# Idle transposes on TensorE around the first score tiles of an attention and two-layer feed-forward kernel

## The chip, the cores and the metric

The kernel runs on one core of a Trainium2 chip. The metric is the device time of one execution in microseconds (us), of which the median of three runs is given. TensorE (PE) does the matmuls, VectorE (DVE), ScalarE (ACT) and GpSimd (POOL) the elementwise work, and SyncE (SP) issues most of the DMAs.

## The reference, cut to what matters

```
q, k, v: (4, 8, 576, 64) f32
q_rot, k_rot = rotate(q), rotate(k)                   # rotary embedding
scores = 1/8 * q_rot @ k_rot.T
attn = exp(scores - max(scores));  attn /= sum(attn)
x = (attn @ v)  as (2304, 512)
g = x @ w_gate                                        # d_ff 1536
x = (silu(g) * (x @ w_val)) @ w_out
g = relu(x @ w_in2) ** 2                              # d_ff 2048
out = g @ w_out2
```

## The kernel before, in words

There are two parts. Part one computes the attention of 32 heads, taken in 16 pairs of heads (a pair is `g`, and `b, j = divmod(g, 4)` its batch and place), and slips in the first chunks of the feed-forward layer as filler matmuls. Part two is the rest of the two feed-forward layers, plain loops of matmuls. The change touches part one only.

For each pair, `add_prep` loads k and q (tile `rot`), multiplies them by the cosine and sine table (L493 for pair 0, L499 for the others) and adds the two halves (L495, L500). `add_kq` splits the rotated k and q into a high part and a rest (L529 to L547 for pair 0, L555 and L557 for the others) and, for pairs after the first, copies them into the operand tiles `kh`, `qa` and `qz` by 13 small DMAs from SP's queue (L569). `add_scores` makes nine score tiles of 128 queries: matmuls of 288 columns into the PSUM tile `s`, of which there are two (L589: four matmuls to each of the tiles 0 to 7, six to tile 8), a maximum on DVE (`nm`, L595), and an exponential on ACT into `p` (L597), which also frees `s`. `add_values` turns `p` by transposes on TensorE (128 x 128, into PSUM tile `pt`, L618), copies them out to `pc` on DVE or ACT (L612, L610), and multiplies by v into the PSUM tile `av`, of which there is one (L652, L655), in two halves: tiles 0 to 3, then 4 to 8. Then come the division by the sum and the split of x for the feed-forward layer. The filler matmuls are L730, the unpacking of the weights L237 to L242.

The order in which each engine does all this is written out ahead of time by a list scheduler inside the kernel, `Plan.order`. Each piece of work is added with an engine, an assumed duration, what it reads and writes, and a rank. At each step the lowest rank that is ready goes next on its engine, where ready goes by the assumed durations. On TensorE every piece has a mode, 0 for score tiles and fillers and 1 for transposes and the product with v, and `STAY` is added to the rank of a piece whose mode is not the last one's: as it is negative, this favours alternating. `Plan.order` also keeps an account of the TensorE clock: it doubles the assumed duration of a piece on TensorE unless enough columns (`COLUMNS`) were counted in the tick before. The chip then runs each engine's list in order, waiting only for real data.

A rank is the pair's number plus `rk(name, g)`, which adds `RANK[name]`, for the first pairs `RANK0` (g < 4) and `RANK1` (g < 2), and for pairs 0 and 1 an entry such as `s0` or `s1`.

Of the kernel before, what the change touches and what calls it, by code (L numbers as in the profile page):

```python
# [18 lines left out]
NR = 64  # L19


RANK = dict(ld=204.044, rope=131.839, k=-43.228, lo=-160.592, dup=314.157, v=-3.533, s=-129.888, mx=-88.9, ex=261.988, pt=-38.854, hi=266.287, av=521.86, rec=59.628, x=402.058, out=453.471, fin=-509.939, scale=-72.768, w=-420.559, dw=352.51, fill=-125.25, sp=-470.346, wl=-348.575, dwl=322.979, df=2.639, r01=-1095.946, r11=-1461.728, r00=-1011.214, r10=-1194.454, k00=-943.413, o00=-768.952, l00=-1080.687, q00=-1037.859, m00=-1368.159, z00=-979.186, k01=-1295.916, o01=-849.303, l01=-1007.3, q01=-1150.876, m01=-747.26, z01=-1157.79, k10=-1334.655, o10=-963.986, l10=-785.158, q10=-957.376, m10=-1162.732, z10=-508.046, k11=-1305.768, o11=-882.245, l11=-858.73, q11=-571.838, m11=-1040.058, z11=-893.411, c0=-569.247, c1=-938.134, rope1=392.215, k1=55.939, lo1=73.053, dup1=-319.318, s0=113.672, s1=262.807, mx0=-214.829, mx1=-239.888, ex0=-79.738, ex1=169.647, pt0=125.887, pt1=-295.963, hi0=103.851, hi1=38.71, av0=492.403, rec0=-133.459, x0=59.381, out0=101.915, scale0=371.475, fin0=-57.497, v1=-56.063)
SHARE = (1,)
RANK0 = dict(rope=-3.842, hi=-1.283, rec=-0.102, out=1.765, scale=3.431, av=6.868, ld=-3.342, dup=0.135, fin=4.672, v=1.694, x=1.078, csq=-0.229, mx=-16.145, k=0.021, lo=5.707, s=-4.387)
RANK1 = dict(ld=2.027, rope=-0.905, k=-15.778, lo=-1.529, v=0.489, s=-520.975, mx=1.596, ex=1.472, pt=-1.685, hi=-4.396, av=0.978, rec=0.97, x=-3.819, fin=-5.258, scale=0.809, csq=4.36)
PB = 10
PC = 6
QB = 4
# [19 lines left out]
class Plan:  # L48
# [7 lines left out]
    HOP = 200  # L56
    HOPS = {("ACT", "DVE"): 152, ("DVE", "ACT"): 128, ("ACT", "PE"): 227, ("ACT", "Pool"): 170, ("Pool", "ACT"): 170, ("Pool", "DVE"): 170}
    SWITCH = 0
    STAY = -578.97

    def __init__(self, places):
        self.places = dict(places)
# [130 lines left out]
def tile_attention_moe_moe2(  # L193
# [13 lines left out]
    nc = tc.nc  # L207
# [147 lines left out]
    with ExitStack() as p1:  # L355
# [8 lines left out]
        plan = Plan(places)  # L364
# [28 lines left out]
        def pe(cols):  # L393
            return cols / 2.4 + 14
# [176 lines left out]
        def add_scores(g):  # L571
            P = pair[g]
            P["p"] = [buf("p", [128, S], bufs=PB) for _ in range(NT)]
            P["sums"] = sums = ssum[g % 2]
            kh, kl, qa, qz = P["kh"], P["kl"], P["qa"], P["qz"]
            for x in range(NT):
                t, h = divmod(x, 2)
                at = g + x / NT
                ps, nm, p = buf("s", [128, 2, 512], bufs=2, pool=pp), buf("nm", [128, 1], bufs=8, pool=sm), P["p"][x]
                for i in range(2):  # L580
                    def mm(i=i, t=t, h=h, ps=ps):
                        c = slice(i * HS, (i + 1) * HS)
                        if t < 4:
                            (_, qc), (_, zc) = (q_at(h, t * 128, t * 128 + 128, z)[0] for z in (NR, 0))
                            prods = [(qa()[:, qc], kh()[:, h, c]), (qz()[:, zc], kl()[:, c])]
                        else:
                            prods = [(qa()[:, NM:NM + 128], kh()[:, 0, c]), (qa()[:, S:S + 128], kh()[:, 1, c]), (qz()[:, NM:NM + 128], kl()[:, c])]
                        for y, (a, w) in enumerate(prods):
                            nc.tensor.matmul(ps()[:, i, :HS], lhsT=a, rhs=w, start=y == 0, stop=y == len(prods) - 1)  # L589
                    nq = {int(t * 128 >= HS), int(min(t * 128 + 127, S - 1) >= HS)}  # L590
                    hs_ = (h,) if t < 4 else (0, 1)
                    rd = [(qa, (h_, y, n)) for h_ in hs_ for y in range(2) for n in nq] + [(qz, (h_, n)) for h_ in hs_ for n in nq]
                    rd += [(kh, (h_, y, i)) for h_ in hs_ for y in range(2)] + [(kl, (h_, i)) for h_ in range(2)]
                    plan.add("PE", pe(HS) * (2 if t < 4 else 3), mm, rd, [ps], at + rk("s", g), cols=HS * (2 if t < 4 else 3))
                plan.add("DVE", 755, lambda ps=ps, nm=nm: nc.vector.tensor_reduce(  # L595
                    out=nm(), in_=ps()[:, :, :HS], axis=AX.XY, op=ALU.max, negate=True), [ps], [nm], at + rk("mx", g))
                plan.add("ACT", 930, lambda x=x, ps=ps, nm=nm, p=p: nc.scalar.activation(  # L597
                    p().rearrange("p (a b) -> p a b", a=2), ps()[:, :, :HS], AF.Exp,
                    bias=nm(), accum_out=sums()[:, x:x + 1]), [ps, nm], [p, (sums, x)], at + rk("ex", g), hold=-100)
# [159 lines left out]

        add_prep(0)  # L760
        add_kq(0)
        for g in range(1, NG):
            add_prep(g)
        for g in range(NG):
            if g:
                add_kq(g)
            add_scores(g)
            add_values(g)
            if g // NP < NSP:
                add_spill(g)  # L770
# [158 lines left out]
```

## Time and profile before

| what | value |
|---|---|
| median of three runs | 1136.91 us (1135.49 to 1137.95) |
| profiled execution: its own time | 1136.43 us |
| profiled execution: its span | 1134.5 us |
| PE busy | 1106.2 us, 98% of the span |
| DVE, ACT, POOL busy | 591.1, 474.4, 482.3 us |
| first and last score matmul start | 12.1 us, 327.3 us |

The span is the stretch from the first to the last instruction of the profiled execution; its own time is 1.9 us more. A matmul's time in a row is from its start to its end in the pipeline, so rows of consecutive matmuls overlap: how fast they follow each other is read from the differences of their starts. "Idle before" is the time for which an engine had nothing running, and the releaser named is what ended it.

### The profile page before, as it was taken

The page shows a single profiled execution, that of the slowest core. Times are in us where ns is not written, and L with a number is a line of the kernel's source. Part 1 is how long each engine was busy: PE and PEld are TensorE (multiplying, and loading weights), DVE is VectorE, ACT ScalarE, POOL GpSimd, SP SyncE. Part 2 cuts the span into 40 slices and gives each one's busy share as a digit, 9 for nine tenths or more (in the row PEclk, how much of TensorE's full clock was granted, in tenths as well). Part 3 has the DMA queues.
Part 4 walks back from the last instruction along what each step waited for, and adds up shares of the span by engine and source line. Part 5 has one row for each costly group of instructions (what it writes and reads, how often), then busy time and mean ns, then how long its engine had stood idle before and what let it go on. Part 6 is the DMA issues. An engine that isn't in the chain of part 4 may idle for free.

```text
span 1134.5 us, 16644 instructions
## 1 busy us (share of the span) xinstructions
PE 1106.2 (98%) x6348; PEld 929.3 (82%) x6348; DVE 591.1 (52%) x974; ACT 474.4 (42%) x985; POOL 482.3 (43%) x380
## 2 busy tenths in 40 slices
PE   4999999999999999999999999999999999999998
PEld 4777788888878888888888888888888888888887
DVE  8778787776664647446355373551144246233212
ACT  6776676666554423122132133443352224223121
POOL 6986784855115324123132145652252234224121
PEclk9999999999999999999999999999999999999999
DMA  9866667564419413012021030120031012000112
GB/s 301 229 194 184 178 166 216 146 158 134 109 49 355 130 45 93 19 32 81 1 75 38 12 101 1 44 68 1 19 94 38 1 57 75 1 1 1 66 29 75
DMA packets 61248, 102.44 MB, mean 90 GB/s; under 512 B 11120, under 2 KB 37488, under 8 KB 60272
## 3 DMA queue, kind: packets, MB, share of 16 engines
q1 hardware_dynamic: 59904, 96.46, 28.5%
q0 software_dynamic: 576, 4.19, 1.0%
q8 instruction: 50, 0.82, 0.3%
q10 hardware_dynamic: 688, 0.72, 0.2%
q14 instruction: 30, 0.25, 0.1%
HBM read 67.17 MB, written 12.06 MB: 70 GB/s over the span
## 4 chain that ended last, share of the span: by engine, by line
PE 89%; DMA 3%; POOL 2%; SPq 2%; DVE 1%; ACT 1%; issue 1%; ACTq 0%; POOLq 0%; DVEq 0%
PE mm L279 23%; PE mm L278 23%; PE mm L280 23%; PE s L589 6%; PE av L652 5%; PE pt L618 5%; PE mm L730 3%; SPq L569 2%; POOL rot L499 1%; DMA qa<-rot 1%; POOL rot L500 1%; ACT p L597 1%; PE av L655 1%; PE pt L674 0%; DMA cs<-in_rope_dram 0%
## 5 line engine op out<-in xcount | busy, mean ns | idle before, releaser
L293 POOL TENSOR_TENSOR h<-s,h 128x512 fp32r<-128x512 f32 (+1 forms) x80 | 96.2, 1203 | 181.5 <-ACT h L292 181.4
L293 POOL TENSOR_TENSOR h<-hf,h 128x512 fp32r<-128x512 f32 (+1 forms) x54 | 66.9, 1238 | 150.7 <-ACT h L292 150.6
L312 DVE TENSOR_TENSOR s<-r,mm 128x512 f32<-128x512 f32 (+1 forms) x80 | 50.6, 633 | 146.6 <-POOL h L293 75.2
L589 PE MATMUL s<-kh,qa 128*128 128x288 f32 x320 | 104.5, 351 | 22.2 <-DVE qa L547 12.1
L595 DVE TENSOR_REDUCE nm<-s 128x1 f32<-128x576 f32 x144 | 106.2, 752 | 15.9 <-PE s L589 13.1
L279 PE MATMUL mm<-wo,h 128*128 128x512 f32 (+1 forms) x292 | 111.5, 386 | 0.0
L618 PE MATMUL pt<-ident,p 128*128 128x128 f32 (+1 forms) x720 | 108.7, 274 | 1.6 <-ACT pc L610 1.1
L597 ACT ACTIVATE p<-s,nm 128x576 f32<-128x576 f32 x144 | 105.5, 734 | 11.2 <-DVE nm L595 8.8
L278 PE MATMUL mm<-wo,h 128*128 128x512 f32 (+1 forms) x292 | 110.1, 386 | 0.0
L280 PE MATMUL mm<-wo,h 128*128 128x512 f32 (+1 forms) x292 | 93.9, 386 | 0.0
L310 ACT ACTIVATE r<-mm 128x512 f32<-128x512 f32 (+1 forms) x80 | 43.9, 549 | 119.2 <-PE mm L280 118.5
L242 POOL TENSOR_TENSOR wi<-wa,wi 128x512 fp32r<-128x512 f32 x36 | 47.2, 1312 | 108.0 <-ACT wi L241 108.0
L618 PEld LDWEIGHTS pt<-ident,p 128*128 128x128 f32 (+1 forms) x720 | 86.4, 135 | 8.1 <-ACT pc L610 1.9
L589 PEld LDWEIGHTS s<-kh,qa 128*128 128x128 f32 x320 | 60.2, 195 | 35.5 <-ACT p L597 16.2
L301 DVE SCALAR_TENSOR_TENSOR th<-th,mm 128x512 f32<-128x512 f32 (+1 forms) x54 | 33.9, 627 | 105.6 <-ACT th L299 105.5
L589 PE MATMUL s<-kl,qz 128*128 128x288 f32 x288 | 85.0, 302 | 0.0
L239 DVE SCALAR_TENSOR_TENSOR wp<-wa,wp 128x512 uint32<-128x512 uint32 x62 | 53.4, 862 | 57.9 <-ACT wa L237 57.8
L292 ACT ACTIVATE h<-s 128x512 fp32r<-128x512 f32 (+1 forms) x80 | 47.2, 590 | 77.3 <-DVE s L312 77.3
L652 PE MATMUL av<-pc,v 128*64 128x256 f32 x640 | 76.1, 384 | 0.0
L612 DVE COPY pc<-pt 128x512 f32<-128x512 f32 (+1 forms) x96 | 64.7, 686 | 21.8 <-PE pt L618 21.6
L292 ACT ACTIVATE h<-hf 128x512 fp32r<-128x512 f32 (+1 forms) x54 | 31.5, 584 | 98.5 <-DVE hf L304 98.0
L280 PE MATMUL mm<-h,wo 128*128 128x512 f32 (+1 forms) x200 | 72.6, 369 | 0.0
(216 smaller groups left out, 2814.9 us busy)
## 6 DMA issues: line engine op xcount, KB each, us to landing
raw<-in_moe_w_out_dram SPq DMA_DIRECT2D x26, 512.0 KB, 3.5
rot<-in_k_dram SPq DMA_DIRECT2D x15, 576.0 KB, 5.0
rot<-in_q_dram SPq DMA_DIRECT2D x15, 576.0 KB, 3.8
kh<-rot SPq DMA_DIRECT2D x60, 144.0 KB, 2.6
raw<-in_moe_w_in_dram SPq DMA_DIRECT2D x16, 512.0 KB, 3.6
raw<-in_moe_w_gate_dram SPq DMA_DIRECT2D x10, 512.0 KB, 3.5
raw<-in_moe_w_val_dram SPq DMA_DIRECT2D x10, 512.0 KB, 3.5
qa<-rot SPq DMA_DIRECT2D x30, 144.0 KB, 2.7
```

Source lines behind the costliest of these rows:

```text
L239: lambda: nc.vector.scalar_tensor_tensor(out=p(), in0=a(), scalar=3, in1=p(), op0=ALU.logical_shift_left, op1=ALU.bitwise_or),
L278: nc.tensor.matmul(ps, lhsT=ah, rhs=bh, start=first, stop=False)
L279: nc.tensor.matmul(ps, lhsT=ah, rhs=bl, start=False, stop=False)
L280: nc.tensor.matmul(ps, lhsT=al, rhs=bh, start=False, stop=last)
L292: nc.scalar.activation(h[:, 0, :n], hf[:, :n], AF.Copy)
L293: nc.gpsimd.tensor_tensor(out=h[:, 1, :n], in0=hf[:, :n], in1=h[:, 0, :n].bitcast(F32), op=ALU.subtract)
L589: nc.tensor.matmul(ps()[:, i, :HS], lhsT=a, rhs=w, start=y == 0, stop=y == len(prods) - 1)
L595: plan.add("DVE", 755, lambda ps=ps, nm=nm: nc.vector.tensor_reduce(out=nm(), in_=ps()[:, :, :HS], axis=AX.XY, op=ALU.max, negate=True), [ ...
L597: plan.add("ACT", 930, lambda x=x, ps=ps, nm=nm, p=p: nc.scalar.activation(p().rearrange("p (a b) -> p a b", a=2), ps()[:, :, :HS], AF.Exp ...
L612: nc.vector.tensor_copy(dst()[:kk], pt()[:kk, :n])
L618: nc.tensor.matmul(pt()[:kk, off + n * 128:off + n * 128 + 128], lhsT=p()[:, c * 128:c * 128 + kk], rhs=ident, is_transpose=True)
L652: nc.tensor.matmul(av()[h * 64:h * 64 + 64, 0:256], lhsT=vt()[:, h, c], rhs=pcs[c]()[:, h * 256:h * 256 + 256], start=c == 0, stop=c == 4)
```

## The change

Two things change. First, `add_idle` adds transposes on TensorE whose results nobody reads. Seven pieces of four of them (28) have the rank -1e5, so they go first on TensorE; they read the first part of pair 0's k tile (`src`), so they can start when that part has been multiplied (L493), and they write one of the two `s` slots. After each of the first four maxima (the loop is over `range(4)`), two pieces of two transposes (16 in all) are listed, writing the `av` slot; the maximum is named as what they read for the order alone, as no operand of theirs is that tile. Second, all ranks are other numbers, some entries of `RANK0` and `RANK1` are gone or new, and `STAY` goes from -578.97 to -439.551, so the order on every engine may differ throughout part one.

```diff
-RANK = dict(..., rope=131.839, s=-129.888, mx=-88.9, pt=-38.854, ..., s0=113.672, s1=262.807, mx0=-214.829, ..., pt0=125.887, pt1=-295.963, rope1=392.215, ...)
+RANK = dict(..., rope=103.217, s=-108.397, mx=-81.407, pt=-50.164, warm=-28.837, ..., s0=119.219, s1=304.557, mx0=-196.999, ..., pt0=139.231, pt1=-361.862, rope1=347.578, ...)
 SHARE = (1,)
-RANK0 = dict(rope=-3.842, ..., mx=-16.145, ..., s=-4.387)
-RANK1 = dict(..., rope=-0.905, ..., s=-520.975, mx=1.596, ..., pt=-1.685, ...)
+RANK0 = dict(rope=50.938, ..., s=-1.154, ex=-1.301)
+RANK1 = dict(..., rope=-0.45, ..., s=-0.067, ex=-3.837, pt=-3.587, ...)
+WARM = 2
...
-    STAY = -578.97
+    STAY = -439.551
...
+                P.setdefault("nm", []).append(nm)
...
         add_prep(0)
         add_kq(0)
+
+        idle = buf("s", [128, 2, 512], bufs=2, pool=pp), buf("av", [128, 512], pool=pp)
+        src = pair[0]["rot"][1]
+
+        def add_idle(t, n, rd, rank):
+            def mm():
+                for i in range(n):
+                    out = idle[t]()[:, 128 * (i % 4):128 * (i % 4) + 128] if t else idle[t]()[:, 0, 128 * (i % 4):128 * (i % 4) + 128]
+                    nc.tensor.matmul(out, lhsT=src()[:, 0, 0:128], rhs=ident, is_transpose=True)
+            plan.add("PE", 110 * n, mm, [(src, 0)] + rd, [idle[t]], rank, mode=1, cols=256 * n)
...
             add_scores(g)
+            if g == 0:
+                for i in range(7):
+                    add_idle(0, 4, [], -1e5)
+                for x in range(4):
+                    for i in range(WARM):
+                        add_idle(1, 2, [pair[0]["nm"][x]], x / NT + RANK["s"] + RANK0["s"] + RANK["warm"])
             add_values(g)
```

## Rows read from the trace of the kernel before

**Rows 1.** Page, busy time of each engine (share of the span) and instructions.
```profile
PE 1106.2 (98%) x6348; PEld 929.3 (82%) x6348; DVE 591.1 (52%) x974; ACT 474.4 (42%) x985; POOL 482.3 (43%) x380
```

**Rows 2.** Waits of PE: engine, line, releaser; us in total, times, longest.
```profile
PE s L589 <- DVE qa L547: 12.1, 1, 12.1
PE s L589 <- ACT p L597: 9.7, 15, 2.4
PE pt L618 <- ACT pc L610: 1.1, 2, 0.8
```

**Rows 3.** Windows by stage: length, then busy us (instructions) of each engine.
```profile
12.13:20.06 7.93, 4.77 (x17) 3.92 (x17) 7.48 (x12) 5.41 (x15) 6.45 (x4) 1.00 1.10 351
20.06:26.00 5.94, 5.94 (x24) 5.61 (x25) 5.35 (x9) 4.51 (x11) 4.92 (x4) 1.00 1.05 269
26.00:60.00 34.00, 31.11 (x255) 24.84 (x255) 25.66 (x47) 26.83 (x65) 32.56 (x22) 1.00 0.84 231
60.00:100.00 40.00, 38.46 (x347) 32.27 (x343) 30.67 (x54) 26.26 (x66) 29.10 (x19) 1.00 0.64 185
100.00:200.00 100.00, 96.18 (x798) 79.87 (x796) 78.22 (x134) 69.38 (x169) 69.14 (x50) 1.00 0.64 185
200.00:300.00 100.00, 99.41 (x787) 83.56 (x786) 69.08 (x129) 64.65 (x156) 57.80 (x43) 1.00 0.53 142
300.00:400.00 100.00, 100.00 (x653) 83.72 (x652) 60.27 (x103) 48.43 (x102) 34.25 (x32) 1.00 0.48 166
```

**Rows 4.** Timeline of PE, 12 to 54 us: start, duration, operation.
```profile
12.54 0.44 PE L589 MATMUL s<-kl,qz 128*128 128x288 f32 x1
12.78 0.44 PE L589 MATMUL s<-kh,qa 128*128 128x288 f32 x1
...
25.62 0.44 PE L589 MATMUL s<-kh,qa 128*128 128x288 f32 x1
25.86 0.36 PE L589 MATMUL s<-kl,qz 128*128 128x288 f32 x1
26.06 1.04 PE L618 MATMUL pt<-ident,p 128*128 128x128 f32 x8
...
28.90 0.37 PE L589 MATMUL s<-kh,qa 128*128 128x288 f32 x1 [0.34 <-ACT rs L661]
...
53.06 0.29 PE L589 MATMUL s<-kl,qz 128*128 128x288 f32 x1
53.19 0.29 PE L589 MATMUL s<-kh,qa 128*128 128x288 f32 x1
```

**Rows 5.** Chain that ended last, 12 to 27 us: start, duration, what.
```profile
12.13 2.32 PE s L589 x8
...
14.47 0.77 DVE nm L595
...
16.15 1.59 DVE rot L500
...
18.38 0.77 DVE nm L595
...
19.17 0.84 ACT p L597 x2
...
20.06 2.62 PE s L589 x8
22.68 1.71 PE pt L618 x8
...
26.23 0.88 PE pt L618 x8
```

**Rows 6.** Timeline of all engines, 5 to 12 us.
```profile
5.19 0.76 DVE L493 TENSOR_TENSOR rot<-rot,cs 128x576 f32<-128x576 f32 x1 [1.48 <-DMA rot<-in_k_dram]
...
11.62 0.45 DVE L547 SCALAR_TENSOR_TENSOR qa<-av,qa 64x288 fp32r<-64x288 f32 x1
```

More of the change, by code (lines that the diff above doesn't have):

```diff
@@ L19 @@
 NR = 64
-RANK = dict(ld=204.044, rope=131.839, k=-43.228, lo=-160.592, dup=314.157, v=-3.533, s=-129.888, mx=-88.9, ex=261.988, pt=-38.854, hi=266.287, av=521.86, rec=59.628, x=402.058, out=453.471, fin=-509.939, scale=-72.768, w=-420.559, dw=352.51, fill=-125.25, sp=-470.346, wl=-348.575, dwl=322.979, df=2.639, r01=-1095.946, r11=-1461.728, r00=-1011.214, r10=-1194.454, k00=-943.413, o00=-768.952, l00=-1080.687, q00=-1037.859, m00=-1368.159, z00=-979.186, k01=-1295.916, o01=-849.303, l01=-1007.3, q01=-1150.876, m01=-747.26, z01=-1157.79, k10=-1334.655, o10=-963.986, l10=-785.158, q10=-957.376, m10=-1162.732, z10=-508.046, k11=-1305.768, o11=-882.245, l11=-858.73, q11=-571.838, m11=-1040.058, z11=-893.411, c0=-569.247, c1=-938.134, rope1=392.215, k1=55.939, lo1=73.053, dup1=-319.318, s0=113.672, s1=262.807, mx0=-214.829, mx1=-239.888, ex0=-79.738, ex1=169.647, pt0=125.887, pt1=-295.963, hi0=103.851, hi1=38.71, av0=492.403, rec0=-133.459, x0=59.381, out0=101.915, scale0=371.475, fin0=-57.497, v1=-56.063)
+RANK = dict(ld=266.609, rope=103.217, k=-71.922, lo=-121.552, dup=290.295, v=-4.733, s=-108.397, mx=-81.407, ex=245.346, pt=-50.164, hi=245.344, av=547.774, rec=71.245, x=424.624, out=467.891, fin=-561.114, scale=-47.957, w=-392.821, dw=372.062, fill=-81.894, warm=-28.837, sp=-461.97, wl=-361.177, dwl=282.317, df=1.537, r01=-1092.467, r11=-1446.233, r00=-1003.515, r10=-1189.886, k00=-885.638, o00=-720.876, l00=-1064.211, q00=-1050.669, m00=-1405.58, z00=-937.259, k01=-1301.078, o01=-883.226, l01=-1012.299, q01=-1188.735, m01=-773.34, z01=-1175.691, k10=-1380.365, o10=-989.529, l10=-837.872, q10=-963.626, m10=-1107.964, z10=-509.852, k11=-1312.706, o11=-905.109, l11=-834.448, q11=-598.424, m11=-1078.001, z11=-921.738, c0=-592.291, c1=-1015.196, rope1=347.578, k1=38.235, lo1=126.821, dup1=-313.591, s0=119.219, s1=304.557, mx0=-196.999, mx1=-202.947, ex0=-117.024, ex1=188.027, pt0=139.231, pt1=-361.862, hi0=99.135, hi1=4.594, av0=463.518, rec0=-119.0, x0=50.457, out0=80.282, scale0=378.987, fin0=-57.894, v1=-1.865)
@@ L23 @@
 SHARE = (1,)
-RANK0 = dict(rope=-3.842, hi=-1.283, rec=-0.102, out=1.765, scale=3.431, av=6.868, ld=-3.342, dup=0.135, fin=4.672, v=1.694, x=1.078, csq=-0.229, mx=-16.145, k=0.021, lo=5.707, s=-4.387)
-RANK1 = dict(ld=2.027, rope=-0.905, k=-15.778, lo=-1.529, v=0.489, s=-520.975, mx=1.596, ex=1.472, pt=-1.685, hi=-4.396, av=0.978, rec=0.97, x=-3.819, fin=-5.258, scale=0.809, csq=4.36)
+RANK0 = dict(rope=50.938, rec=6.702, scale=0.088, av=4.54, ld=-2.517, fin=-3.654, v=-1.701, csq=-1.713, k=-10.823, lo=-0.514, s=-1.154, ex=-1.301)
@@ L26 @@
+RANK1 = dict(ld=10.234, rope=-0.45, k=0.033, lo=5.593, s=-0.067, ex=-3.837, pt=-3.587, hi=6.221, rec=-2.021, x=-0.024, out=-0.768, fin=1.52, scale=10.873, csq=1.491)
+WARM = 2
 PB = 10
```

## Prediction

> **What bounds the kernel.** I read the page's busy times first, then PE's waits, then the span cut into stages, then PE's timeline and the chain of waits up to the point where PE is never idle again. TensorE is busy 1106.2 of 1134.5 us [rows 1], so 28.3 us are all that a better order could win at full speed. Of these 12.1 are the one wait before the first score tile, and 9.7 are waits of score tiles for an exponential (ACT p), which frees a score slot [rows 2]. The stages show where they lie [rows 3]: PE is idle 3.16 us between 12.13 and 20.06, 2.89 between 26 and 60, 1.54 between 60 and 100, 3.82 in the next 100 us, 0.59 in the next, and none between 300 and 400. So from about 300 us on the end is set by how much work TensorE still has, and what is won earlier is kept if PE doesn't wait for it again on the way.
>
> The second thing to see is speed. The granted clock is printed as 1.00 in every stage [rows 3], but the starts say otherwise: early on, score matmuls of 288 columns follow each other by 12.78 - 12.54 = 0.24 us, 1.2 columns per ns, and so still at 25.62 to 25.86; at 53 us the same matmul follows by 0.13 us, 2.2 per ns [rows 4]. That is the level of 1.2 GHz up to about 26.0 us and the level of 2.4 GHz after. Eight transposes tell the same: 1.71 us from 22.68, 0.88 us from 26.23 [rows 5], that is 0.214 and 0.110 us for one. Before the rise TensorE had been busy without a break since 20.06 us, 5.94 us in 5.94 [rows 3].
>
> **The idle transposes ahead of the first tile.** They can start when k's first part is multiplied, 5.19 + 0.76 = 5.95 us, plus a hop as from DVE's L547, which ends at 12.07, to PE's first matmul at 12.13 [rows 5, 6]: 0.06. So 6.0 us. 28 x 0.214 = 6.0 us at the low level, so they end at 12.0 us at the latest, before the first score tile could start (12.13). They cost nothing: what hides them is PE's 12.1 us wait. Without that cover they would cost 6.0 us; if the start slips by more than 0.13 us, the rest of the slip comes on the first tile. Score slot: they hold one of two, but TensorE itself is the next to write it, in order, so no other engine is waited for.
>
> What they are worth depends on the clock. The nearest row is the rise in this trace, 5.94 us after the start of unbroken work; 5.94 after 6.0 is 11.95 us, just ahead of the first tile. Ends: the clock is at the high level from the first tile on, or rises where it did before, at 26.0. I take the first. The unbroken work that preceded the rise held eight transposes, 1.7 us out of 5.9 [rows 5], and eight unbroken score matmuls alone (2.32 us from 12.13) hadn't raised it. So transposes at least don't break the run that raises the clock.
>
> **The gain, stage by stage.** From 20.06 to 26.00 PE is busy all the time at the low level; at the high level the same work takes half: 5.94 / 2 = 2.97 us less. From 12.13 to 20.06 PE is busy 4.77 of 7.93 us but DVE 7.48 [rows 3], so this stage goes by DVE's list, and faster matmuls alone win no more than DVE's idle 0.45 us. But the list can change: the chain runs from a maximum to the second addition of pair 1's rotation (L500, 16.15, which holds DVE until about 18.1) and only then to the next maximum at 18.38 [rows 5]. That maximum ranks ahead of the addition (after: mx -81.4 - 197.0 = -278.4 against rope 103.2 + 50.9 - 0.5 + 347.6 + 1 = 502.3), so it is second only because its scores come too late for the slot at 16.15. Matmuls at half the time bring them about 0.4 us earlier, which is what decides. Then the maximum comes up to 18.38 - 16.15 = 2.2 us earlier, and with it the exponential and PE's restart at 20.06. Ends 0 and 2.2; I take 1.0, in the middle, since DVE and ACT have the later copies and exponentials to do in less time too.
>
> **The idle transposes behind the maxima.** 16 x 0.110 = 1.76 us, at the low level 3.42. In the trace of before the places behind the first four tiles hold 3.16 us of idle PE, two waits for ACT p, the longest 2.4 [rows 2, 3]. Nothing on the chip makes them wait for the maximum, they only stand in PE's queue, with the next score tile behind them. I take four of them, behind the fourth maximum, as being in the way: 0.44 us. Ends 0 and 1.76. What waits for a tile held up so is DVE's next maximum. They also hold the only av slot, which the first product with v needs much later.
>
> **The new ranks and STAY.** In the trace of before I have no price for another order. The bound below is the PE idle time from 20 to 300 us, 8.8 us [rows 3], of which an order could win or double some. I take 0, as nothing says that this order waits more or less.
>
> **Sum.** -2.97 - 1.0 + 0.44 = -3.5 us. The profiled execution's own 1136.43 becomes 1132.9; it lies 0.5 below the median of 1136.91, so against the median the forecast is 1133.4 us.
>
> At this point the Trainium skill speaks against the change. Its page TensorE: Matmul & The Clock Gate, section Part 4: PE-mode transpose, says of transposes that full rate "doesn't engage" for them, as they don't count as busy in the same way. By that rule the idle transposes would raise nothing, and the sum would be +0.44 x 2 = +0.9 us instead of -3.5. This trace shows transposes running at 0.110 us after the rise, so the level holds for them; whether transposes alone raise it no row shows.
>
> **The rivals.**
> *The clock doesn't rise from transposes alone.* Then the first tiles run at the low level as before, four idle transposes are in the way at 0.214 us, +0.86, and the time is 1137.8 against the median, within 0.2%. For it: before the rise, transposes were never alone. Against it: they were part of the unbroken run. A variant, that the level falls again in the DVE-bound stage, gives about the same; in this trace 2.89 us of idle PE between 26 and 60 us [rows 3] had not lowered it at 53 us. Chance 0.14.
>
> *Full conversion.* PE is fed as fast as it can go: all 10.71 us of low-level work halve, 5.36, and the 3.16 us of idle time go too, 8.5 us: 1128.4. Against it: DVE is 94% busy in the first stage. Chance 0.08.
>
> *Supply eats it.* From 26 to 60 us POOL, which rotates the later pairs, is busy 32.56 of 34 us, and DVE and ACT together 52.5 of 68 [rows 3]; pair 1's first tile can't start before its copies have landed (28.90 in before, [rows 4]). If PE is three us ahead and waits for these, the gain goes to waits before 60 us and the time is 1135 to 1137. For it POOL's 96%; against it, POOL works one to two pairs ahead by then. Chance 0.15.
>
> *Slower: transposes ahead of score tiles in pairs 0 and 1.* In before a score tile of pair 0 ranks at -129.9 - 4.4 - 521.0 + 113.7 = -541.6 and a transpose group at 85.3, 627 apart, more than STAY, so tiles always go first. After, they are at 9.6 and 85.5, 76 apart, less than STAY's 440, so they alternate; in pair 1 transposes (-415.6) go ahead of tiles (194.9) always, where before tiles led by 56. Five groups of four, 5 x 0.44 = 2.2 us, come before the last tiles of each half, and behind the last tile maximum and exponential (0.77 + 0.84 [rows 5]) are bare with nothing else to do: up to 3.8 us a pair, 7.6 for two, against 3.5 won: +4.1, or 1141.0. It decides for slower where PE's waits for ACT p before 100 us grow by more than 3.5 + 2.3 us. Against it: the same transposes must be done anyway, and the next pair's tiles fill in when landed. Chance 0.13.
>
> **How the numbers follow.** The forecast's case has 0.50 (its own range 1130.5 to 1134.6), full conversion 0.08, supply 0.15, no rise 0.14, slower 0.13. What measurement can tell from no change is about 0.2%, 2.3 us. Faster: 0.50 and 0.08, less 0.02 for the edge of the first, 0.56. Same: 0.15, 0.14 and the 0.02, 0.31. Slower 0.13. The range takes the forecast, supply and no rise whole and parts of the outer two: 1129.5 to 1138.3.
>
> **What would show it.** Right: 28 transposes from 6.0 us, the first score matmuls 0.13 us apart, PE restarting on the fifth tile at 18 to 19 us, the first product with v some 3 us earlier than before, and PE's waits from 20 to 300 us still near 9 us. Wrong: starts 0.24 us apart past 13 us (no rise); the first tile later than 12.3 (cover gone); waits for ACT p or copies between 26 and 100 us grown by about what was won (supply), or by more (the slower rival). I would be furthest off if the new order changes the waits between 60 and 300 us, for which I have no price.

## The result: slower by 0.5%

The changed kernel takes 1142.53 us (median of five runs, 1141.60 to 1144.92) against 1136.49 us for the kernel before in the same session (five runs, 1135.49 to 1137.95). The ratio is 1.0052 with a 95% interval of 1.0038 to 1.0065. The forecast was 1133.4 us, with 1138.3 as the upper end. The profiled execution of the changed kernel took 1142.01 us, its span 1140.2. Line numbers after the change are one or two higher than before (L495 is now L496, L589 is L590, L618 is L620); the idle transposes are L772.

The page's busy times, as [rows 1]:

```profile
PE 1113.3 (98%) x6392; PEld 936.3 (82%) x6392; DVE 591.4 (52%) x966; ACT 476.9 (42%) x994; POOL 482.2 (42%) x379
```

Two of the waits of PE, as [rows 2]; the two others that matter, 6.0 us ahead of the transposes and 2.8 us for the copy `pc`, stand in the timeline below:

```profile
PE s L590 <- DVE qa L548: 5.8, 1, 5.8
PE s L590 <- ACT p L599: 5.0, 12, 1.0
```

The windows by stage, as [rows 3] (length, PE, PEld, DVE, ACT, POOL, then granted clock, DMA share and GB/s):

```profile
12.13:20.06 7.93, 3.65 (x16) 3.64 (x17) 7.64 (x12) 4.33 (x11) 5.00 (x3) 0.72 0.82 250
20.06:26.00 5.94, 5.71 (x36) 5.20 (x35) 5.02 (x10) 4.83 (x13) 3.92 (x3) 0.80 0.60 143
26.00:60.00 34.00, 28.09 (x209) 22.57 (x208) 28.58 (x40) 22.39 (x54) 25.66 (x15) 0.90 0.78 233
60.00:100.00 40.00, 38.28 (x329) 32.21 (x330) 30.41 (x56) 30.20 (x74) 35.50 (x26) 1.00 0.71 198
100.00:200.00 100.00, 97.95 (x804) 81.30 (x803) 73.20 (x129) 67.78 (x166) 68.83 (x47) 1.00 0.67 186
200.00:300.00 100.00, 99.71 (x816) 84.72 (x814) 69.27 (x130) 70.00 (x171) 56.89 (x41) 1.00 0.55 150
```

TensorE does start its transposes at 6.0 us, but then stands for another 5.8 us, because the first score tile is late. The span is 5.7 us longer, and it splits so. Idle time of PE from 12.13 to 60 us is 10.42 us (4.28, 0.23 and 5.91) against 6.05 in [rows 3], 4.4 more. From 60 to 300 us it is 4.06 against 5.95, 1.9 less. PE's busy time is 7.1 us longer [rows 1], of which 4.6 are the 28 transposes in what was a wait, so 2.5 more. That makes 5.0; the rest, 0.7, lies in waits after 300 us (PE is busy 99.21 us from 300 to 400, 100.00 in [rows 3]). The 2.5 are, by an estimate from the rows below, the 16 transposes behind the maxima (16 x 0.11 = 1.8 us) and 0.8 us from more work at the low clock level. The loss is therefore for the most part ahead of 60 us, in two waits, and not where the new ranks had most room, from 60 to 300 us.

The timeline of PE, as [rows 4]:

```profile
6.00 4.60 PE L772 MATMUL s<-ident,rot 128*128 128x128 f32 x28 [6.00 <-DVE rot L494]
16.41 0.61 PE L590 MATMUL s<-kh,qa 128*128 128x288 f32 x1 [5.81 <-DVE qa L548]
...
17.29 0.44 PE L590 MATMUL s<-kl,qz 128*128 128x288 f32 x1
17.53 0.44 PE L590 MATMUL s<-kh,qa 128*128 128x288 f32 x1
...
23.44 0.29 PE L590 MATMUL s<-kh,qa 128*128 128x288 f32 x1
23.58 0.29 PE L590 MATMUL s<-kl,qz 128*128 128x288 f32 x1
...
40.43 0.66 PE L620 MATMUL pt<-ident,p 128*128 128x128 f32 x4 [2.78 <-ACT pc L612]
```

And the windows cut where the granted clock steps (the same columns):

```profile
8.78:15.60 6.82, 1.81 (x17) 1.57 (x15) 6.78 (x7) 4.07 (x11) 6.10 (x3) 1.00 1.08 361
15.60:22.43 6.83, 6.02 (x26) 5.97 (x27) 6.16 (x12) 3.86 (x10) 2.87 (x3) 0.50 0.41 127
22.43:42.91 20.48, 16.34 (x119) 13.18 (x118) 17.75 (x29) 15.34 (x39) 13.20 (x9) 1.00 0.80 239
42.91:49.74 6.83, 6.23 (x28) 5.59 (x27) 5.30 (x10) 4.30 (x12) 6.83 (x5) 0.50 0.89 233
```

So the transposes do what they are for: the granted clock goes to the high level (2.4 GHz) at 8.78 us, when TensorE had done nothing but idle transposes from 6.00 on: 13 of them start in the 2.78 us up to there, 0.21 us apart, and the other 15 in the 1.6 us after it, 0.11 apart. Then it is spent on nothing. The 28 transposes end at 10.6, TensorE stands until 16.41, the clock falls at 15.60, and the first tiles run at the low level after all (17.29 to 17.53, 0.24 us apart). It rises again at 22.43 (23.44 to 23.58, 0.14 apart), and falls a second time at 42.91, after the wait of 2.78 us that ends at 40.43 and shorter ones. From 12.13 us on, busy time at the low level is 6.02 and 6.23 us, together 12.25, against 10.71 in [rows 3]: in the changed kernel the clock doesn't win anything, it loses about half of the difference, 0.8 us (an estimate: the same transposes were 0.21 us apart at the low level and 0.11 at the high one).

### Why the first tile is late

The lines of DVE and POOL in the timeline after the change:

```profile
9.50 0.65 POOL L510 COPY gate<-rot 128x1 f32<-128x1 f32 x1 [6.43 <-DVE rot L494]
10.02 0.46 DVE L496 TENSOR_TENSOR mm<-rot 128x288 f32<-128x288 f32 x1
10.11 2.83 POOL L500 TENSOR_TENSOR rot<-rot,cs 128x1152 f32<-128x1152 f32 x1
10.39 2.87 DVE L496 TENSOR_TENSOR av<-rot 128x288 f32<-128x288 f32 x1
12.90 2.83 POOL L500 TENSOR_TENSOR rot<-rot,csq 128x1152 f32<-128x1152 f32 x1
13.29 0.92 DVE L544 TENSOR_TENSOR kl<-pt,kh 64x288 fp32r<-64x288 f32 x2
14.14 1.73 DVE L538 CAST qz<-qa 64x224 fp32r<-64x224 f32 x1
15.90 0.94 DVE L548 SCALAR_TENSOR_TENSOR qa<-av,qa 64x288 fp32r<-64x288 f32 x2
```

and before:

```profile
9.90 0.45 DVE L495 TENSOR_TENSOR av<-rot 128x288 f32<-128x288 f32 x1
10.04 0.73 POOL L509 COPY gate<-rot 128x1 f32<-128x1 f32 x1 [6.96 <-DVE rot L493]
10.27 0.45 DVE L495 TENSOR_TENSOR mm<-rot 128x288 f32<-128x288 f32 x1
10.73 2.63 POOL L499 TENSOR_TENSOR rot<-rot,cs 128x1152 f32<-128x1152 f32 x1
```

Pair 0's q is rotated in two parts; part one lands in `av`, part two in `mm`, and the first tile needs part one. Two of the new ranks change places: `r00` (q's part one, -1011.2 to -1003.5) and `l01` (a rest of k, -1007.3 to -1012.3). In the new lists part two of q is multiplied and added first. GpSimd's little copy `gate`, which is there to hold its rotations back, reads part two; so it fires at 9.50 instead of 10.04, and GpSimd's rotation of pair 1 starts at 10.11, before DVE's last addition. That addition takes 2.87 us instead of 0.45: it ends at 13.26, when the rotation's 2.83 us from 10.11 are over (12.94). The CAST at 14.14, beside the second rotation, is longer too (1.73 us, 0.41 before). Of the first tile's delay of 4.3 us, 2.5 come with the additions, of which the last ends at 13.26 instead of 10.72, and 1.7 with this CAST: the new list has it ahead of the subtraction `qa` (15.90) that the first tile waits for, the old one behind (the subtraction at 11.62 [rows 6], the CAST at 13.08). The two subtractions at 13.29, which read PSUM and SBUF, take 0.46 each beside the same rotation and aren't held. The page GPSIMD Engine Reference of the Trainium skill, section 1. Specifications, says that GpSimd shares its SBUF interfaces with VectorE and that the contention is with instructions of two SBUF inputs or in a 2-port mode; this trace agrees for the addition, with 2.87 against 0.45 us.

### Why pair 2 is late

Lines of SP, POOL and ACT in the timeline after the change:

```profile
21.04 1.17 SPq L570 DMA_DIRECT2D kh<-rot  x2
...
27.47 0.53 SPq L484 DMA_DIRECT2D rot<-in_k_dram  x1
...
31.89 2.65 POOL L500 TENSOR_TENSOR rot<-rot,cs 128x1152 f32<-128x1152 f32 x1 [5.72 <-DMA rot<-in_k_dram]
...
39.23 0.67 ACT L238 ACTIVATE wa<-h 128x512 f32<-128x512 f32 x1 [2.42 <-POOL w L243]
39.80 0.57 ACT L612 ACTIVATE pc<-pt 64x512 f32<-64x512 f32 x1
```

and before:

```profile
13.16 0.47 SPq L483 DMA_DIRECT2D rot<-in_k_dram  x1
...
23.95 2.66 POOL L499 TENSOR_TENSOR rot<-rot,cs 128x1152 f32<-128x1152 f32 x1
```

SP issued the load of pair 2's k at 13.16 us before, and at 27.47 now, behind most of pair 1's copies, which begin at 21.04 and wait for data themselves. The idle transposes behind the maxima read pair 0's k tile, one of four `rot` slots, and pair 2's load needs that slot; for the planner it is taken until the last of them, so it lists the load later. Two kernels with newly planned lists show that this slot alone decides (h0 and h2 below): they differ in one thing, that in h2 the transposes behind the maxima read the table `cs` instead. SP's timeline of h0, then of h2:

```profile
27.68 0.53 SPq L484 DMA_DIRECT2D rot<-in_k_dram  x1
```

```profile
12.64 0.88 SPq L484 DMA_DIRECT2D rot<-in_k_dram  x1
```

In the changed kernel POOL stands 5.72 us for it and starts pair 2's rotation at 31.89 instead of 23.95. What follows is a chain over in-order queues: POOL's weight subtraction (L243) comes behind the rotations, ACT's next weight step (39.23) waits 2.42 us for it, and the copy `pc` stands behind that step, though its own data are there. TensorE waits 2.78 us for that copy at 40.43.

### The profile page after: what moved, and what is told of

It is laid out like the page before. It is cut to its first block, busy times and chain, and to the rows that moved or that the text cites. A ratio compares the mean times of both kernels' runs of the same rounds, so it can differ in the third digit from the quotient of the medians.

```text
span 1140.2 us, 16712 instructions
## 1 busy us (share of the span) xinstructions
PE 1113.3 (98%) x6392; PEld 936.3 (82%) x6392; DVE 591.4 (52%) x966; ACT 476.9 (42%) x994; POOL 482.2 (42%) x379
## 4 chain that ended last, share of the span: by engine, by line
PE 89%; POOL 3%; DMA 2%; DVE 2%; ACT 1%; SPq 1%; issue 1%; ACTq 0%; POOLq 0%; DVEq 0%
PE mm L281 23%; PE mm L280 23%; PE mm L279 23%; PE s L590 6%; PE av L654 5%; PE pt L620 5%; PE mm L732 4%; POOL rot L500 1%; SPq L570 1%; ACT p L599 1%; DMA qa<-rot 1%; PE av L657 1%; POOL rot L501 1%; PE pt L676 0%; DVE nm L597 0%
## 5 line engine op out<-in xcount | busy, mean ns | idle before, releaser
L590 PE MATMUL s<-kh,qa 128*128 128x288 f32 x320 | 103.3, 348 | 11.4 <-DVE qa L548 5.8
L620 PE MATMUL pt<-ident,p 128*128 128x128 f32 (+1 forms) x720 | 109.9, 275 | 3.8 <-ACT pc L612 2.8
L620 PEld LDWEIGHTS pt<-ident,p 128*128 128x128 f32 (+1 forms) x720 | 86.5, 135 | 10.8 <-ACT pc L612 3.0
L243 POOL TENSOR_TENSOR wi<-wa,wi 128x512 fp32r<-128x512 f32 x36 | 47.2, 1310 | 108.0 <-ACT wi L242 108.0
L590 PE MATMUL s<-kl,qz 128*128 128x288 f32 x288 | 84.6, 302 | 0.0
L590 PEld LDWEIGHTS s<-kh,qa 128*128 128x128 f32 x320 | 60.4, 195 | 23.1 <-ACT p L599 10.6
L281 PE MATMUL mm<-h,wo 128*128 128x512 f32 (+1 forms) x200 | 72.6, 369 | 0.0
L280 PE MATMUL mm<-h,wo 128*128 128x512 f32 (+1 forms) x200 | 72.6, 368 | 0.0
```

The source lines that it names most:

```text
L280: nc.tensor.matmul(ps, lhsT=ah, rhs=bl, start=False, stop=False)
L281: nc.tensor.matmul(ps, lhsT=al, rhs=bh, start=False, stop=last)
L620: nc.tensor.matmul(pt()[:kk, off + n * 128:off + n * 128 + 128], lhsT=p()[:, c * 128:c * 128 + kk], rhs=ident, is_transpose=True)
```

## The experiments

e3 and h0 to h3 let the planner write new lists; all others keep its finished lists of one kernel and add, leave out or move single pieces in them. None changes what is computed.

**Is it the order or the transposes?** e1 keeps the changed kernel's lists and emits no transposes, e4 keeps the lists of before and adds the 28.

```diff
 e1, from the kernel after
-                for i in range(n):
+                for i in range(0):
 e4 and i1, from the kernel before, behind the multiplication of k's first part (L493)
+ for k_ in range(28):
+     nc.tensor.matmul(t[:, 0, 128 * (k_ % 4):128 * (k_ % 4) + 128], lhsT=x()[:, 0, 0:128], rhs=ident, is_transpose=True)
```

> The changed kernel's lists, in which the idle transposes emit nothing; all else stays in place. Theory: the loss comes from the new order at the opening (DVE adds q's second part first, which lets GpSimd start pair 1's rotation, and DVE's addition for q's first part then stands 2.5 us behind GpSimd); then the first score tile still starts at 16.0 to 16.7 us and the time is 1141 to 1145 us. Rival, the transposes themselves cost the time (in the way, and a clock that falls again): 1135 to 1138 us.

> The kernel before, its lists untouched, with 28 transposes ahead of the first score tile. If transposes alone raise the clock and it lasts: first tile at 12.1, score matmuls 0.13 us apart from there, 1133 to 1135.5 us. If it falls again between 13 and 20 us, where DVE sets the pace: 1135.5 to 1137 us. Rival (transposes harm): 1138 us or more.

e1: 1141.46 us, ratio 1.0040 (1.0020 to 1.0061). First tile at 17.3 us, POOL's wait for pair 2's k 5.96 us. Without a single idle transpose most of the loss stands (4.8 of 6.0 us): it is the order in the lists. That order still has the transposes planned in, so it contains what they do to the planner, the late load above.

e4: 1135.66 us, ratio 0.9991 (0.9981 to 1.0000). The same kernel with more runs, i1:

> The kernel of e4 again, in more rounds. If the 1 us is real: ratio 0.9985 to 0.9998 to the kernel before, interval clear of 1. If it was chance: 0.9998 to 1.0010.

i1: 1136.08 us, ratio 0.9994 (0.9985 to 1.0003). The 28 transposes alone make no difference that this measurement can tell, though the clock was at the high level from 11.50 to 14.92 us in e4 and from 11.69 to 18.52 in i1. e4's trace shows where the faster tiles end, in PE's timeline:

```profile
28.49 0.50 PE L595 MATMUL s<-kh,qa 128*128 128x288 f32 x1 [2.45 <-DMA qa<-rot]
```

The fifth tile starts at 18.16 us instead of 20.06, but pair 1's first tile waits 2.45 us for its copies to land; in before it started at 28.90 [rows 4]. Behind this wait the clock, which was high from 21.75 us on, is low again from 28.57 to 31.98, where before has it high from 26.0 on. Those copies take, in the DMA issues from 10 to 28 us (KB each, median us to landing), first of e4 and then of the changed kernel, whose pair 2 loads aren't in the queue beside them (4.9 us in the kernel before):

```profile
kh<-rot SPq DMA_DIRECT2D x4, 144.0 KB, 6.3
```

```profile
kh<-rot SPq DMA_DIRECT2D x4, 144.0 KB, 2.5
```

In i1 TensorE waits for no copy. There the first product with v comes at 29.42 us, 1.05 earlier than before (30.47), and PE then idles 4.87 us between 26 and 60 us instead of 2.89 [rows 3].

**The opening.** f3 takes the lists of before and does only the swap: q's part two multiplied and added first. f1 takes the changed lists and undoes it, with the later steps of part one. e2 was an earlier try that moved additions and roundings but not the multiplications, e3 the kernel before with one rank changed (`l01`).

```diff
 f3, on the finished list of before (mul and add of q: name, q or k, part)
+for a, where, b in [(('mul', 0, 1), 'before', ('mul', 0, 0)), (('add', 0, 1), 'before', ('add', 0, 0))]:
+    a, b = self.named[a], self.named[b]
+    out.remove(a)
+    out.insert(out.index(b) + (where == "behind"), a)
 f1, on the finished list of after; e2 is the same without the first entry
+for a, where, b in [(('mul', 0, 0), 'before', ('mul', 0, 1)), (('add', 0, 0), 'before', ('add', 0, 1)), (('q', 0, 0), 'before', ('q', 1, 0)),
...
 e3, ranks of before
-l01=-1007.3
+l01=-1012.299
```

> The changed kernel with seven pieces moved in the lists so that q's first part is added, rounded and split ahead of its second, as in the kernel before; nothing else moves and all transposes stay. Theory (opening): first score tile back at 12 to 12.8 us, clock high in the first tiles, 1133 to 1138 us. Rival (the rest of the new order is worse by itself, between 26 and 60 us): first tile early, but 1139 us or more.

> The kernel before with one rank changed (l01 = -1012.299 as in the changed kernel), no transposes: the opening takes the changed kernel's order on DVE. Theory (opening): the first score tile starts at 15.5 to 16.7 us and the time is 1139 to 1142 us. Rival (transposes, or the rest of the order): 1135.5 to 1138 us.

> The kernel before, its lists as they are and no transposes, with only q's second part multiplied and added ahead of its first on DVE (four pieces). Theory: GpSimd starts pair 1's rotation one multiplication (0.7 us) earlier, DVE's last addition stands behind it for over 2 us, the first tile starts at 14.5 to 16.5 us, and the time is 1138.5 to 1142 us. Rival (a late first tile is made up for later, as PE waits there anyway): 1136 to 1138 us.

> The changed kernel's lists as they are, with only the opening moved by hand (q's first part multiplied, added, rounded and split ahead of its second on DVE and ACT, as before), all transposes kept; unlike e2 the multiplication is moved too, so that GpSimd's start, which hangs on the second part's multiplication, no longer falls ahead of DVE's last addition. Theory (the late first tile is the loss): first tile at 12.1 to 13 us and 1136 to 1139 us. Rival (pair 2's loads, still late, hold the rest): first tile early and 1140 to 1143 us.

e2: 1144.25 us, ratio 1.0068 (1.0051 to 1.0085), a miss that names the cause. Both additions came behind GpSimd's start and were held, the second for 2.87 us from 13.90, beside the rotation from 13.63; the first:

```profile
11.06 2.60 POOL L506 TENSOR_TENSOR rot<-rot,cs 128x1152 f32<-128x1152 f32 x1
11.09 2.90 DVE L501 TENSOR_TENSOR av<-rot 128x288 f32<-128x288 f32 x1
```

What counts is the order of the multiplications, since the gate reads one of them. e3: 1146.75 us, ratio 1.0089 (1.0073 to 1.0104), first tile 16.8 us: the one rank makes the whole opening (addition 2.87 us, CAST 1.62 us). But the planner made other lists everywhere, so its time says little about the opening alone. f3 does: 1138.18 us, ratio 1.0014 (1.0004 to 1.0024), first tile 14.12 us, and its addition is held in the same way:

```profile
9.69 2.69 POOL L507 TENSOR_TENSOR rot<-rot,cs 128x1152 f32<-128x1152 f32 x1
9.84 2.87 DVE L502 TENSOR_TENSOR av<-rot 128x288 f32<-128x288 f32 x1
```

Swapping two multiplications and two additions makes the first tile 2.0 us late, as the CAST stays behind, and costs 1.7 us. The way is not the obvious one: the first product with v comes at 30.47 us, just as before. What is late is GpSimd's later work (below). f1, the other way round: 1141.20 us, ratio 1.0034 (1.0022 to 1.0045), first tile at 12.42. It wins back only 1.3 of the 4.3 us: TensorE now waits 2.63 us at 17.05 for an exponential, and pair 2 is as late as before (POOL waits 6.0 us, PE 2.7 us for `pc`).

**Pair 2's loads, and the 16 transposes.** f2 is f1 with pair 2's loads ahead of pair 1's copies on SP, and the later transposes read the table `cs` so that this is free. g1 does that alone, without the opening. g2 is f2 without the 16 transposes behind the maxima.

```diff
 f2 and g1, on the finished list of after
+for i in (1, 0):
+    out.remove(self.named["ld", 2, i, 0])
+    out.insert(out.index(dups[0]), self.named["ld", 2, i, 0])
...
-nc.tensor.matmul(out, lhsT=src()[:, 0, 0:128], rhs=ident, is_transpose=True)
+nc.tensor.matmul(out, lhsT=(cs() if t else src())[:, 0, 0:128], rhs=ident, is_transpose=True)
 g2, from f2
-                for i in range(n):
+                for i in range(0 if t else n):
```

> f1, and pair 2's two loads moved ahead of pair 1's copies on SP, with the transposes behind the maxima reading the cosine table so that nothing holds k's slot. Theory: GpSimd's wait of 5.7 us for pair 2's k is gone, and the time is 1133 to 1137 us, 1 to 4 us under f1. If the late loads cost nothing: as f1 within 1 us.

> The changed kernel's lists with pair 2's two loads moved ahead of pair 1's copies (the transposes behind the maxima read the cosine table), the opening left late. If the two faults add: 2.1 us under the changed kernel, 1139.5 to 1141.5 us. If the late first tile hides the late loads: as the changed kernel, 1142 to 1143.5 us.

> f2 with the 16 transposes behind the maxima left out and the 28 ahead kept. If the 16 in the way are what is left: 1136 to 1138 us, 1.5 us or more under f2. If the rest of the new order is: 1138.5 to 1140 us, as f2.

f2: 1139.08 us, ratio 1.0017 (1.0002 to 1.0031); POOL's wait for k is gone. g1: 1140.70 us, ratio 1.0031 (1.0021 to 1.0041). g2: 1137.11 us, ratio 1.0006 (0.9996 to 1.0015). From the changed kernel to f1, f2 and g2 the medians go 1142.5, 1141.2, 1139.1, 1137.1: the opening 1.3 us, the loads 2.1 (alone 1.8), the 16 transposes 2.0, together 5.4 of the 6.0 us lost. Intervals of neighbours overlap, so a single step is less sure than the sum; the changed kernel against f2, and f1 against g2, stand apart, and g2 can't be told from the kernel before.

f2 shows something else, in the window from the first step of its clock to the next:

```profile
12.24:39.55 27.31, 20.87 (x147) 16.85 (x147) 24.26 (x42) 22.21 (x55) 23.84 (x14) 1.00 0.88 269
```

All of pair 0's tiles at the high level, the first product with v at 27.29 us, 3.2 earlier than before, as the prediction wanted it; in g2, where the clock is low from 17.32 to 24.15, it is at 28.40. And f2 is no faster than before. At 39.55 us its clock falls, for 3.4 us, where before has it high. Its profiled execution is the fastest of its ten (1136.80 us), so the trace doesn't show what the others lose against g2.

**Can transposes in the gaps pay?** i2 and f4 add to the 28 some in the waits that [rows 2] show as ACT p: 8 ahead of the third tile, and in f4 16 ahead of the fifth as well.

```diff
 f4, from e4; i2 has {2: 8}
-                    def mm(i=i, t=t, h=h, ps=ps):
+                    def mm(i=i, t=t, h=h, ps=ps, fill={2: 8, 4: 16}.get(x, 0) if g == 0 and i == 0 else 0):
```

> e4 (the kernel before with 28 transposes ahead) and 8 more ahead of the third tile and 16 ahead of the fifth, reading the cosine table, to keep the clock high through PE's two waits. If pair 1's copies set the pace (they land at 28.5 us in e4): score matmuls 0.13 us apart from 12 to 26 us, and 1134.5 to 1136.3 us, not 0.7 us under e4. If the clock is what holds the gain back: 1132 to 1134.3 us.

> f4 with only the 8 transposes ahead of the third tile. If transposes in a wait are free and the 16 ahead of the fifth tile were in the way: as e4, 1135 to 1136.5 us. If any transposes in the gaps upset the lists: 1138 to 1141 us.

f4: 1141.35 us, ratio 1.0039 (1.0020 to 1.0058). i2: 1137.80 us, ratio 1.0014 (1.0005 to 1.0022). f4's clock, in one window:

```profile
9.11:29.59 20.48, 14.49 (x104) 12.47 (x104) 17.96 (x34) 17.45 (x42) 18.93 (x12) 1.00 1.07 322
```

Every tile of pair 0 at the high level, and TensorE still idle 5.99 us of 20.48, with DMA full and pair 1's first tile at 28.61 us, as before. The 8 cost 1.7 us against i1 and are 0.9 us of work; the 24, 2.6 us of work, cost 5.3. The intervals of i1 stand apart from both. In the traces PE is busy 95.3 (f4) and 95.4 us (i2) from 100 to 200 us, 96.7 in i1 and 96.18 in [rows 3]: about 1.4 us of the cost lie there. Why that stage waits more isn't settled. One thing is left untested: the added transposes also take one of the two `pt` slots each time, and no run separates that from their length.

**Can the supply be moved?** If the copies are held up by the weights loaded beside them, loading these behind the copies should let pair 1 in earlier. g3 does so with the 28 transposes, g4 without.

```diff
 g3 and g4, on the finished list: four weight loads behind the copy of pair 1 that the program adds last
+for a, where, b in [(('wl', 2), 'behind', ('duplast', 1)), (('wl', 3), 'behind', ('wl', 2)), ...]:
```

> e4 (the kernel before with 28 transposes ahead) and four weight loads of 512 KB, which stood around pair 1's copies on SP, moved behind them. If copies that land late hold back what the clock wins: pair 1's first tile at 25 to 27 us in place of 28.5, and 1132.5 to 1135 us. If not: 1135 to 1137 us.

> The control of g3: the same four loads moved, no transposes. The first tiles run at the low level, TensorE is itself busy until 28 us, so earlier copies are of little use: 1135.5 to 1137 us. If the loads alone are the gain: as g3.

g3: 1140.18 us, ratio 1.0032 (1.0022 to 1.0043). g4: 1141.02 us, ratio 1.0036 (1.0023 to 1.0049). The copies land in 2.8 us instead of 6.3, pair 1's first tile comes at 25.78 us and the first product with v at 27.40. Then it is all given back at once, in g3's timelines of POOL and PE:

```profile
41.73 2.61 POOL L513 TENSOR_TENSOR rot<-rot,csq 128x1152 f32<-128x1152 f32 x1 [4.56 <-DMA qz<-rot]
```

```profile
46.95 0.48 PE L637 MATMUL pt<-ident,p 128*128 128x128 f32 x1 [5.26 <-ACT pc L629]
```

POOL waits 4.56 us for the q of pair 3, ACT for POOL, and TensorE 5.26 us for ACT's copy `pc`. g4 has the same wait (5.68 us) without any transposes, so it belongs to the loads. But not all of pair 1's copies are ahead of the weights: the copy that the program adds last isn't the last in the list, and a small one, issued at 27.39 us in g3, still stands behind the four weight loads. Its row in g3's DMA issues (KB, us to landing):

```profile
qa<-rot SPq DMA_DIRECT2D x1, 16.0 KB, 9.2
```

It reads pair 1's q, and pair 3's q needs that slot: SP waits for it and issues the load at 36.65 us (35.26 in before; in g4 at 39.43, behind a copy that takes 10.6 us). So g3 and g4 show what one late copy costs. They don't show that the supply can't be moved.

**Where a gain or a loss ahead of 30 us goes.** All kernels with the lists of before pass through that place. The columns are, from their timelines: start of the first product with v; start of POOL's multiplication of pair 3's q, with its wait for DMA; restart of PE behind `pc`, with its wait; start of pair 1's first product with v; span, all in us.

| kernel | first v | POOL, pair 3 | PE behind pc | pair 1's v | span |
|---|---|---|---|---|---|
| before | 30.47 | 40.11 (1.00) | 45.58 (0.81) | 49.10 | 1134.5 |
| i1 | 29.42 | 39.69 (2.48) | 45.13 (1.42) | 48.66 | 1133.8 |
| f3 | 30.47 | 41.66 (1.53) | 47.10 (2.34) | 50.62 | 1135.8 |
| g3 | 27.40 | 41.73 (4.56) | 46.95 (5.26) | 53.04 | 1137.8 |
| g4 | 29.55 | 44.30 (5.52) | 49.52 (5.68) | 55.76 | 1141.2 |

The span doesn't follow the first column at all: g3 leads there by 3.1 us and ends 3.3 late. It goes with the one before the last: -0.4, +1.5, +3.9 and +6.7 us there stand against -0.7, +1.3, +3.3 and +6.7 of span. In i1 and f3 that difference is there already at POOL, whose multiplication waits for pair 3's q in every row, and stays the same through the next two columns: in i1 TensorE is 1.05 us ahead, POOL waits 1.48 us longer, and 0.4 us are left. In g3 and g4 PE restarts 1.4 and 3.9 us late; another 2.6 and 2.7 come behind that restart, where the granted clock is at 0.50 for 6.83 us (from 45.74 in g3, from 48.65 in g4), so that PE needs 6.1 and 6.2 us to pair 1's product with v and 3.5 in the other rows. These are single executions, and the other three kernels with these lists, e4, i2 and f4, follow less closely: +0.6, -0.5 and +0.7 in that column against -0.6, +0.3 and +2.3. So the table shows the way in four kernels, and not a rule for all.

**Ranks mended instead of lists.** h0 gives pairs 0 and 1 the tile rank of before; h1 adds `l01` -990, h2 the table as the transposes' source, h3 both.

```diff
 h0 to h3, RANK1
-s=-0.067
+s=-520.975
```

> The changed kernel with one entry changed, RANK1's s = -520.975 as in the kernel before, so that score tiles of pairs 0 and 1 rank ahead of transposes again. Base for the next three. Theory (two faults of the new order: q's second part first at the opening, and pair 2's loads behind pair 1's copies on SP, because the idle transposes behind the maxima hold the slot of pair 0's k): both are still there, so first tile at 16 to 17 us, GpSimd idle for about 5 us ahead of pair 2's rotation, 1140 to 1144 us. Rival of the prediction (transposes ranked ahead of tiles): 1134 to 1138 us.

> h0 with l01 = -990, which puts q's first part first on DVE and ACT as in the kernel before; pair 2's loads still behind pair 1's copies. Theory: first tile at 12.1 to 12.5 us, GpSimd still idle ahead of pair 2's rotation; 1136 to 1139 us, 3 to 5 us under h0. If only the loads matter: as h0.

> h0 with the idle transposes behind the maxima reading the cosine table in place of pair 0's k, so that k's slot is free and pair 2's loads stand ahead of pair 1's copies; the opening stays as in the changed kernel. Theory: first tile still at 16 to 17 us, GpSimd's wait for pair 2's k gone, 1137 to 1141 us, 2 to 4 us under h0. If only the opening matters: as h0.

> h0 with both mended. Theory (the two faults are the loss): 1133 to 1136.5 us, at or a little under the kernel before, and not below 1133, as pair 1's copies don't land before 28 us whatever TensorE does. Rival (some third part of the new ranks costs as much): 1138 us or more.

All four missed in time: 1154.70, 1160.03, 1159.39 and 1154.37 us, ratios 1.0157, 1.0205, 1.0206 and 1.0160, each within 0.0029. The pieces that were meant did move: the first tile comes at 16.65 us in h0, 13.18 in h1, 16.52 in h2 and 13.04 in h3, and the load of pair 2's k at 27.68, 24.73, 12.64 and 13.24 us. The loss is spread over 100 to 400 us (PE is busy 93.65 of 100 us from 300 to 400 in h3 and 89.51 in h1, 100.00 in [rows 3]). One rank gives another order everywhere, so these times tell nothing about the part that was meant. They show how much hangs on one rank: h0 is 12.2 us slower than the changed kernel, h1 5.3 slower than h0, and e3 10.1 slower than the kernel before, each by one number.

## Why the prediction was wrong

Measured from the kernel before, -3.5 us were forecast and +6.0 came, 9.5 apart. By the medians of the experiments 4.0 of these are gain that didn't come, 1.3 the opening, 2.1 the loads of pair 2 and 1.6 the 16 transposes beyond their 0.44; 0.6 remain.

**The new ranks, "I take 0".** This step failed. The prediction had no row for another order and took 0, with the room for waits seen between 20 and 300 us. The order changed the time where it wasn't looked for: ahead of 20 us, where a copy released one multiplication (0.7 us) too early, and a CAST listed ahead, make the first tile 4.3 us late, of which f1 wins back 1.3 us of time. The full diff had the two ranks; the prediction's own sentence that PE's 12.1 us wait hides the transposes took the end of pair 0's preparation as fixed, and that end was part of what the diff moved.

**The transposes' hidden cost.** Of what the idle transposes behind the maxima hold, the prediction named the `av` slot alone. It left out what they read: a slot of the four `rot` tiles, which the planner then gives to pair 2 later. That was worth about 2 us (f2, g1).

**The 16 in the way, +0.44.** The sign was right, the size wrong: g2 against f2 gives 2.0 us, above the 1.76 that the prediction had as its upper end; the intervals of these two overlap, but i2 against i1, which stand apart, points the same way (1.7 us for 8). That they cost it by standing in front of the next tile, as the prediction had it, is not shown.

**The clock, right.** The 28 start at 6.00 and raise the clock by themselves, at 8.78 us; the prediction took 11.95. The prediction's rival that transposes alone raise nothing, with the Trainium skill's page TensorE: Matmul & The Clock Gate, section Part 4: PE-mode transpose, behind it, is refuted by that row: from 6.00 to 8.78 TensorE ran nothing else. Page and trace differ here, and the trace decides. That the level falls again in the first stage was there only as a variant of this rival, with no chance of its own; it happened at 15.60.

**Its worth, -2.97 and -1.0, wrong.** In the changed kernel the low level has more work than before, 12.25 against 10.71 us, so where -2.97 was forecast there is +0.8, by the estimate above. With the lists of before the high level came before the first tile and the fifth tile came 1.9 us earlier, near what was forecast (18 to 19 us). That it came near is luck. The prediction had the third tile's maximum pass the addition of pair 1's rotation, but these lists are written ahead and keep the addition first. What changed is who of VectorE and GpSimd began its half of that addition first, before and then in e4:

```profile
16.07 1.41 POOL L500 TENSOR_TENSOR rot<-rot 128x576 f32<-128x576 f32 x1
16.15 1.94 DVE L500 TENSOR_TENSOR rot<-rot 128x576 f32<-128x576 f32 x1
```

```profile
15.43 0.76 DVE L506 TENSOR_TENSOR rot<-rot 128x576 f32<-128x576 f32 x1
15.63 1.83 POOL L506 TENSOR_TENSOR rot<-rot 128x576 f32<-128x576 f32 x1
```

VectorE is free at 16.19 instead of 18.09 us, and these are the 1.9. They moved the end by 0.6 to 1.0 us at most (i1, e4), which the measurement can't tell from none. The rival "supply eats it" (0.15; 1135 to 1137) describes this outcome, and in e4 its mechanism too, the wait of 2.45 us for copies; in i1 TensorE waits for `p` and `pc` instead, and GpSimd 1.48 us longer for pair 3's q. f2, f4 and g3, each with most or all of pair 0 at the high level, won nothing either, and in the executions profiled the level falls later in all three, at 39.55, 29.59 and 45.74 us, as it does in e4 at 28.57. What this costs is shown for g3 alone; e4, which has it, is no slower than i1, which hasn't. The prediction read from [rows 3] that POOL is busy 96% from 26 to 60 us, and set that aside because POOL works one to two pairs ahead; it should have followed this one queue to TensorE, as in i1 and f3 the end moves with the load that POOL waits for.

**The slower rival, right in sign, not in cause.** Its mark was that PE's waits for ACT p grow; they fell from 9.7 to 5.0 us.

What stays open: why transposes in TensorE's waits cost about twice their own length, a part of it only between 100 and 200 us; what a gain ahead of 30 us would be worth if all of pair 1's copies stood ahead of the weights; and 0.6 of the 6.0 us. No version here is faster than the kernel before by more than can be measured.

## What to carry to other kernels

Before pricing an addition in a wait, ask whether the wait itself stays where it is: a diff that changes a planner's numbers moves the end of the wait too, and the first thing to compare is the order of the preparation that ends it. An instruction that does nothing still reads a buffer, and a planner holds that buffer for it: let it read a constant. And work made faster early in a pipeline won nothing here that can be measured: it met copies, a load or another wait. So look for what the next stage waits for before counting the gain to the end.

## What the runs showed of the hardware

An addition on VectorE with both inputs in SBUF (128 x 288, f32) took 2.87 us instead of 0.45 when it began beside a multiplication of 2.83 us on GpSimd, in the changed kernel, and 2.87 to 2.90 in e2, e3 and f3; each time it ended 0.3 us after GpSimd's. A subtraction reading PSUM took its usual 0.46 beside it. Where VectorE began first, it was GpSimd's addition that grew, from 1.41 us in the kernel before to 1.83 in e4. The same 28 transposes, with nothing ahead of them on TensorE, had the granted clock at the high level 2.8 us after the first of them in the changed kernel, 3.2 in f4, 5.5 in e4, 5.6 in i1 and 6.1 in f2. And copies of 144 KB landed 2.5 us after their issue in the changed kernel (DMA share 0.60 from 20.06 to 26 us), 4.9 us in the kernel before and 6.3 in e4 (both 1.05), so the share alone doesn't tell it.
